# Attention over 32 memory slots and a bilinear FFN on one core: one written list orders every unit, column sums of exp(phi) on VectorE, all blocks in pairs of seven half products

## The chip, the core and the metric

The kernel runs on one core of a Trainium2 chip. A core has five engines with their own instruction streams, each in its own order: TensorE (PE in the profile, with its weight loads as PEld), VectorE (DVE), ScalarE (ACT), GpSimd (POOL) and SyncE (SP). They meet only at semaphores. Transfers between HBM and the on-chip memory (SBUF) run on 16 DMA engines that all queues share. Matrix products land in PSUM, eight banks in all. The metric is the device time in microseconds (us) of one execution; lower is better.

## What is computed

The reference, cut to what matters (8 batches, 8 heads, 576 tokens, head size 64, 32 memory slots, model width 512, inner width 1536):

```python
def _attn_ref(q, k, v, phi):
    a = phi - np.max(phi, axis=2, keepdims=True)
    a = np.exp(a)
    a = a / (np.sum(a, axis=2, keepdims=True) + 1e-09)
    k_m = np.einsum('bhsm,bhsd->bhmd', a, k)
    v_m = np.einsum('bhsm,bhsd->bhmd', a, v)
    scores = (1.0 / np.sqrt(q.shape[-1])) * np.matmul(q, k_m.transpose(0, 1, 3, 2))
    scores = scores - np.max(scores, axis=-1, keepdims=True)
    attn = np.exp(scores)
    attn = attn / (np.sum(attn, axis=-1, keepdims=True) + 1e-09)
    return np.matmul(attn, v_m)

def _moe_ref(x, w_a, w_b, w_out):        # x: the attention's output, 4608 tokens x 512
    return (x @ w_a) * (x @ w_b) @ w_out
```

The sum over tokens of exp(phi), one number for each memory slot, is the divisor of the first softmax. This text calls it the column sum.

## The kernel before

**Chain of a batch.** `exp_phi` (ScalarE) takes exp of phi. TensorE then sums k and v over tokens with these weights (`sums` for batches 0 and 1, line 270; `kv_sums` for batches 2 to 7, line 213). The column sums come out of the same products: `kv_sb` holds three planes, k, v and a third that is filled once with 1/16 (lines 155 and 168), so a product over plane 3 gives the column sum. `take_kv` or `sums` divides, the result is transposed, `scores` multiplies with q, `exp_scores`, `denominators` and `normalise` (later batches: `e_turn`, `token_sums`, `token_normalise`, `a_turn`) make the attention A. `fold` multiplies the v sums into both up weights, so that the FFN's up projections need only A: its PSUM results `pva` are cast into `vab` by `take_fold`.

**Up.** `up_half(b, i, hf, x)` makes one 128 x 288 tile of x @ w_a (x=0, PSUM `pa`, cast by ScalarE into `a_sb`) or of x @ w_b (x=1, PSUM `pb`, multiplied by VectorE with `a_sb` into `ht`). There are 8 x 12 x 2 such pairs. In batch 0 the casts lie in 20 slots of the `w_sums` buffer, which is not yet needed; later in a pool of 4.

**Down.** 36 blocks of 128 tokens are multiplied by `w_out`. The first four (`early_downs`, line 474) are done as they are: 12 products of 512 columns for each block. The other 32 go in 16 pairs (`two_downs`, line 518): a pair is a 2 x 2 block product made from seven half-size products instead of eight, each of 6 matmuls of 256 columns. It takes sums of weights (`sum_weights`, eight GpSimd operations, once) and four sums of tokens for each pair (`sum_tokens`; GpSimd, and VectorE for the last two pairs).

**Order.** The program is scheduled by hand: each engine runs its instructions in the order in which Python emits them. `chain` emits batches 0 and 1 from two strings, `period` attaches the chain units of batch b+1 to the up steps of batch b, and the class `Work` spreads the down matmuls over the up steps at an even rate. `settle` empties a started half product before units that take four banks. `fill` emits dummy products that keep TensorE busy while it has nothing to do: 98 of 128 columns and 10 of 512, all before 19 us. PSUM banks are given out in rotation, oldest first.

**Loads.** All of them but k of batch 0 are issued from GpSimd's queue, in order: phi, q, v of batch 0; the up weights in column ranges 0:256, 256:512, 512:1024, 1024:1536 (`load_wab`, lines 158 to 169); then `o0 p o1 k q0 q1 o2 o3 v0 v1 o4 o5`, that is the down weights in six parts between the loads of batch 1 (line 175). At most eight loads are in flight: an issue waits until the load eight places earlier has landed.

Of the kernel before, what the change touches and what calls it, by code (L numbers as in the profile page):

```python
# [14 lines left out]
CS = 16.0  # L15


@with_exitstack
def kernel(
# [54 lines left out]
    kv_sbs = [consts.tile([P, 3, NHP, NI * D], F16, name=f"kv_sb{t}") for t in range(2)]  # L74
# [80 lines left out]
    nc.vector.memset(kv_sbs[0][:, 2], 1.0 / CS)  # L155
    for x in halves:
        nc.vector.tensor_copy(out=kvs[0][:, 0, x], in_=k_f32[:, x])
    load_wab(0, 256)
    load_wab(256, 512)

    ones = consts.tile([P, 4, 32], F16, name="ones")
    nc.vector.memset(ones, 1.0)
    nc.gpsimd.affine_select(out=ones, in_=ones, compare_op=ALU.is_ge, fill=0.0, base=0,
                            pattern=[[-32, 4], [0, 32]], channel_multiplier=1)
    nc.gpsimd.affine_select(out=ones, in_=ones, compare_op=ALU.is_ge, fill=0.0, base=31,
                            pattern=[[32, 4], [0, 32]], channel_multiplier=-1)
    load_wab(512, 1024)
    nc.gpsimd.memset(kv_sbs[1][:, 2], 1.0 / CS)  # L168
    load_wab(1024, 1536)
    loads = {f"o{n}": lambda n=n: load_wo(n) for n in range(NFF // 2)}  # L170
    loads |= {"p": lambda: load_phi(1), "k": lambda: load_k(1)}
    for n, x in enumerate(halves):
        loads[f"q{n}"] = lambda x=x: load_q(1, x)
        loads[f"v{n}"] = lambda x=x: load_v(1, x)
    for x in "o0 p o1 k q0 q1 o2 o3 v0 v1 o4 o5".split():
        loads[x]()
# [11 lines left out]
    def units(b):  # L188
# [18 lines left out]
        def slot_sums(z):  # L207
            if z == 0:
                t["es"] = kvs[b][:, 2, 0, 0:2 * NHP * M].bitcast(F32).rearrange("p (c m) -> p c m", m=M)
            nc.vector.tensor_reduce(out=t["es"][:, 2 * z:2 * z + 2], in_=t["exp"][:, 2 * z:2 * z + 2].rearrange("p c i m -> p c m i"),  # L210
                                    axis=mybir.AxisListType.X, op=ALU.add)

        def kv_sums():

            given = "es" in t
            n = (3 - given) * D
            t["pkv"] = [banks.take([P, 2 * D + (1 if given else D)], F32, "pkv", hold=True) for _ in range(2)]
            for i in range(NI):
                for g in range(2):
                    for j in range(4):  # L220
                        r, hp = head(g, j)
                        nc.tensor.matmul(  # L222
                            t["pkv"][g][0][32 * j:32 * j + 32, 0:n],
                            t["exp"][64 * r:64 * r + 64, hp, i, :],
                            kvs[b][64 * r:64 * r + 64, 0:3 - given, hp, D * i:D * (i + 1)],
                            start=(i == 0),
                            stop=(i == NI - 1),
                            tile_position=(64 * r, 32 * j),
                        )
            for g in range(2 * given):  # L230
                for j in range(4):
                    r, hp = head(g, j)
                    nc.tensor.matmul(
                        t["pkv"][g][0][32 * j:32 * j + 32, 2 * D:2 * D + 1],
                        t["es"][64 * r:64 * r + 64, hp],
                        one_cs[64 * r:64 * r + 64],
                        start=True,
                        stop=True,
                        tile_position=(64 * r, 32 * j),
                    )  # L240
# [29 lines left out]
        def sums(g, x):  # L270
# [5 lines left out]
            part = (slice(0, 3, 2), slice(1, 2))[x]  # L276
            pk = banks.tile([P, 2 - x, D], F32, name="pk")
            for i in range(NI):
                for j in range(4):
                    r, hp = head(g, j)  # L280
                    nc.tensor.matmul(
                        pk[32 * j:32 * j + 32],
                        t["exp"][64 * r:64 * r + 64, hp, i, :],
                        kvs[b][64 * r:64 * r + 64, part, hp, D * i:D * (i + 1)],
# [4 lines left out]
            if x == 0:  # L289
                nc.vector.reciprocal(out=t["rphi"][:, g:g + 1], in_=pk[:, 1, 0:1])  # L290
            nc.vector.tensor_scalar(out=t["kvm"][:, g, x], in0=pk[:, 0], scalar1=t["rphi"][:, g:g + 1], scalar2=None,
# [12 lines left out]
        def scores(gs):  # L304
            if 0 in gs:
                t["E"] = mid.tile([P, 2, S], F16, name="E")
            if len(gs) > 1 and b > 2:
                work.settle()
# [70 lines left out]
        def fold(lo, hi, zs):  # L379
            if b not in vabs:  # L380
                vabs[b] = [mid.tile([P, 2, d_ff], F16, name=f"vab{x}") for x in range(2)]
            if len(zs) > 1 and b > 2:
                work.settle()
# [64 lines left out]
    def down_part(po, bank, cidx, lo, hi):  # L448
        pair, c = divmod(cidx, NI)
        for i in range(lo, hi):  # L450
            nc.tensor.matmul(po, ht[:, i, P * c:P * (c + 1)], wo_sb[:, i, :],  # L451
                             start=(i == 0), stop=(i == NFF - 1))
            if i == NFF - 1:
                banks.free(bank)
                o_sb = opool.tile([P, d_model], F32, name="o_sb")
                nc.scalar.mul(out=o_sb, in_=po, mul=1.0 / (CS * CS))
                for z in range(2):
                    slot = 2 * c + z
                    nc.sync.dma_start(out=out_rows[2 * pair + slot // NI, slot % NI],
                                      in_=o_sb[64 * z:64 * z + 64, :])  # L460
            yield

    def down(cidx):

        po, bank = banks.take([P, d_model], F32, "po", hold=True)
        yield from down_part(po, bank, cidx, 0, NFF)

    EARLY = 4

    def early_downs():  # L470

        pos = [banks.take([P, d_model], F32, "po", hold=True) for c in range(EARLY)]
        for n in range(NFF // 2):
            for c in range(EARLY):
                yield from down_part(*pos[c], c, 2 * n, 2 * (n + 1))

# [7 lines left out]
    def sum_weights():  # L487
        nc.gpsimd.tensor_copy(out=w_sums[:, 0, 0, 0:1], in_=attn[1][:, 1, S - 1:S])
        t = [w_sums[:, x] for x in range(4)]
        for out, in0, in1 in ((t[0], quarter(0, 1), quarter(0, 0)), (t[1], quarter(1, 1), t[0]),  # L490
                              (t[2], quarter(1, 1), quarter(0, 1)), (t[3], quarter(1, 0), t[1])):
            for x in range(2):
                sl = slice(KH // 2 * x, KH // 2 * (x + 1))
                nc.gpsimd.tensor_tensor(out=out[:, sl], in0=in0[:, sl], in1=in1[:, sl], op=ALU.subtract)
# [7 lines left out]
    def sum_tokens(cidx, engine):  # L502

        h_sums[cidx] = spool.tile([P, 4, KH, P], F16, name="h_sums")
        t = [h_sums[cidx][:, x] for x in range(4)]
        (a11, a12), (a21, a22) = ([tokens_of(cidx + y, x) for x in range(2)] for y in range(2))
        for out, in0, in1, op in ((t[0], a21, a22, ALU.add), (t[1], t[0], a11, ALU.subtract),
                                  (t[2], a12, t[1], ALU.subtract), (t[3], a11, a21, ALU.subtract)):
            engine.tensor_tensor(out=out, in0=in0, in1=in1, op=op)  # L509
            yield  # L510
# [7 lines left out]
    def two_downs(self, cidx):  # L518
        S1, S2, S4, S3 = (h_sums[cidx][:, x] for x in range(4))
# [3 lines left out]
        ends = cidx == PAIRED[-1]  # L523
# [22 lines left out]
        self.brim = True  # L546
# [11 lines left out]
        self.brim = False  # L558
# [7 lines left out]
        self.brim = True  # L566
# [7 lines left out]
        self.brim = False  # L574
# [14 lines left out]
    LEAD = 24  # L589
    PAIRED = range(EARLY, BLOCKS, 2)  # L590

    class Work:


        def __init__(self):
            self.todo = self.products()
            self.ready = self.done = self.summed = 0
            self.owed = self.rate = 0.0
            self.brim = False
            self.sums = self.add_up()  # L600
            self.next_sum = next(self.sums)

        def products(self):
            for cidx in PAIRED:
                yield from two_downs(self, cidx)

        def add_up(self):
            for n, cidx in enumerate(PAIRED):
                for x in range(4):
                    yield n, 7 * KH * n + KH * (x + 1)  # L610
                    if x == 0:
                        sums = sum_tokens(cidx, nc.gpsimd if n < len(PAIRED) - 2 else nc.vector)
                    next(sums)
            while True:
                yield len(PAIRED), 0

        def sum_ahead(self):
            while self.next_sum[0] < self.summed and self.next_sum[1] <= self.done + LEAD:
                self.next_sum = next(self.sums)

        def pull(self, n):
            for _ in range(min(n, self.ready - self.done)):
                self.owed -= 1.0
                self.sum_ahead()
                self.done += 1
                next(self.todo)

        def settle(self):

            while self.brim and self.done < self.ready:  # L630
                self.pull(1)

        def advance(self):
# [162 lines left out]
```

The softmax here doesn't subtract the row's maximum and nothing guards it: scores larger than these inputs give would overflow.

## Time and profile before

| | |
|---|---|
| time, median of 3 runs | 239.33 us (239.0 to 240.5) |
| span of the profiled execution | 237.2 us |
| TensorE busy | 227.1 us, 96% of the span |
| VectorE busy | 169.5 us, 71% |
| ScalarE busy | 153.7 us, 65% |
| GpSimd busy | 155.6 us, 66% |
| DMA | 37.27 MB, mean 157 GB/s |
| TensorE clock granted | 0.998 |

The span runs from the first to the last instruction; the measured time lies 2.1 us above it. TensorE's matmuls are pipelined, so busy time overstates what it does: the distance from one start to the next is the real price of one. Between 60 and 220 us the busy share is 99 to 100%. In that stretch VectorE is busy 13.2 to 16.6 us of each 20 us, ScalarE 12.1 to 16.6.

Durations that matter below, mean of one: `ht` multiply on VectorE 448 ns, `a_sb` cast on ScalarE 410 ns, `h_sums` on GpSimd 1640 to 1670 ns and on VectorE 550 ns, `w_sums` on GpSimd 1633 ns, `vab` casts 606 ns (ScalarE) and 683 ns (VectorE).

### The profile page before, as it was taken

The page shows a single profiled execution, that of the slowest core. Times are in us where ns is not written, and L with a number is a line of the kernel's source. Part 1 is how long each engine was busy: PE and PEld are TensorE (multiplying, and loading weights), DVE is VectorE, ACT ScalarE, POOL GpSimd, SP SyncE. Part 2 cuts the span into 40 slices and gives each one's busy share as a digit, 9 for nine tenths or more (in the row PEclk, how much of TensorE's full clock was granted, in tenths as well). Part 3 has the DMA queues.
Part 4 walks back from the last instruction along what each step waited for, and adds up shares of the span by engine and source line. Part 5 has one row for each costly group of instructions (what it writes and reads, how often), then busy time and mean ns, then how long its engine had stood idle before and what let it go on. Part 6 is the DMA issues. An engine that isn't in the chain of part 4 may idle for free.

```text
span 237.2 us, 7718 instructions
## 1 busy us (share of the span) xinstructions
PE 227.1 (96%) x3064; PEld 167.5 (71%) x3064; DVE 169.5 (71%) x415; ACT 153.7 (65%) x394; POOL 155.6 (66%) x132
## 2 busy tenths in 40 slices
PE   7888998999999999999999999999999999999993
PEld 7545563455756877868777877877878687888882
DVE  4646874368949958969776995779786877766642
ACT  2276761559699589786778458776776777555330
POOL 7954244589979969392799699692939265956001
PEclk9999999999999999999999999999999999999999
DMA  6999999999982999944499857997063342212146
GB/s 231 236 198 206 211 252 207 243 220 275 229 182 50 219 262 252 220 100 92 80 248 238 153 123 171 211 203 99 6 137 59 82 104 37 56 34 67 38 101 155
DMA packets 38436, 37.27 MB, mean 157 GB/s; under 512 B 14688, under 2 KB 32480, under 8 KB 38400
## 3 DMA queue, kind: packets, MB, share of 16 engines
q0 software_dynamic: 19264, 23.14, 52.5%
q1 hardware_dynamic: 18624, 12.85, 24.3%
q10 hardware_dynamic: 512, 0.79, 1.0%
q8 instruction: 24, 0.39, 0.7%
q14 instruction: 12, 0.10, 0.1%
HBM read 42.47 MB, written 9.44 MB: 219 GB/s over the span
## 4 chain that ended last, share of the span: by engine, by line
PE 76%; DMA 14%; POOL 5%; ACT 2%; issue 1%; DVE 1%; DVEq 0%; POOLq 0%
PE py L527 17%; PE pa L655 17%; PE pb L655 17%; PE pv L527 8%; DMA wa_sb<-in_moe_w_a_dram 6%; DMA wo_sb<-in_moe_w_out_dram 6%; PE pva L389 5%; PE px L527 4%; PE po L451 3%; PE pkv L222 2%; DMA kvT<-rep 2%; PE pscore L318 1%; POOL wb_sb L100 1%; POOL wa_sb L99 1%; POOL kv_sb L168 1%
## 5 line engine op out<-in xcount | busy, mean ns | idle before, releaser
L666 DVE TENSOR_TENSOR ht<-a_sb,pb 128x288 f16<-128x288 f16 x168 | 72.3, 448 | 33.5 <-ACT a_sb L663 23.7
L655 PEld LDWEIGHTS <-vab 128*128 128x128 f16 x768 | 73.1, 98 | 22.1 <-issue 5.3
L663 ACT CAST a_sb<-pa 128x288 f16<-128x288 f32 x168 | 65.9, 410 | 30.8 <-PE pa L655 26.4
L655 PE MATMUL pa<-A,vab 128*128 128x288 f16 x384 | 75.8, 286 | 0.0
L655 PE MATMUL pb<-A,vab 128*128 128x288 f16 x384 | 75.3, 286 | 0.1
L509 POOL TENSOR_TENSOR h_sums<-ht 128x768 f16<-128x768 f16 x28 | 46.7, 1670 | 23.1 <-DVE ht L666 23.1
L527 PEld LDWEIGHTS <-h_sums 128*128 128x128 f16 x384 | 36.7, 98 | 9.2 <-issue 3.0
L402 ACT CAST vab<-pva 128x512 f16<-128x512 f32 (+1 forms) x60 | 31.9, 575 | 7.5 <-PE pva L389 7.1
L527 PEld LDWEIGHTS <-ht 128*128 128x128 f16 x288 | 27.9, 98 | 6.1 <-issue 1.3
L527 PE MATMUL py<-w_sums,h_sums 128*128 128x256 f16 x192 | 30.2, 273 | 0.0
L402 DVE CAST vab<-pva 128x512 f16<-128x512 f32 (+1 forms) x44 | 26.7, 635 | 3.7 <-PE pva L389 3.6
L509 POOL TENSOR_TENSOR h_sums<-h_sums,ht 128x768 f16<-128x768 f16 x14 | 23.4, 1668 | 0.9
L509 POOL TENSOR_TENSOR h_sums<-ht,h_sums 128x768 f16<-128x768 f16 x14 | 23.0, 1640 | 0.9
L331 ACT ACTIVATE E<-pscore 128x288 f16<-128x288 f32 x32 | 10.7, 416 | 10.6 <-PE pscore L318 10.5
L527 PE MATMUL pv<-w_sums,h_sums 128*128 128x256 f16 x96 | 16.2, 273 | 0.0
L527 PE MATMUL py<-wo_sb,ht 128*128 128x256 f16 x96 | 16.2, 273 | 0.0
L534 ACT ACTIVATE u<-py 128x256 f32<-128x256 f32 x32 | 12.5, 391 | 5.7 <-PE py L527 5.2
L527 PE MATMUL px<-wo_sb,ht 128*128 128x256 f16 x96 | 15.9, 273 | 0.0
L527 PE MATMUL py<-w_sums,ht 128*128 128x256 f16 x96 | 15.2, 273 | 0.1
L527 PE MATMUL pv<-wo_sb,h_sums 128*128 128x256 f16 x96 | 14.4, 273 | 0.0
L196 ACT ACTIVATE exp_sb<-phi_sb 128x576 f16<-128x576 f32 x16 | 10.9, 699 | 5.2 <-DMA phi_sb<-in_phi_dram 5.2
L205 DVE STREAM_TRANSPOSE qT<-q_sb 128x288 f32<-128x288 f32 x32 | 14.1, 460 | 0.2 <-DMA q_sb<-in_q_dram 0.2
(71 smaller groups left out, 264.7 us busy)
## 6 DMA issues: line engine op xcount, KB each, us to landing
out_dram<-o_sb SPq DMA_DIRECT2D x68, 128.0 KB, 3.0
phi_sb<-in_phi_dram POOLq DMA_DIRECT2D x8, 576.0 KB, 7.9
kv_sb<-in_v_dram POOLq DMA_DIRECT2D x7, 576.0 KB, 11.2
kv_sb<-in_k_dram POOLq DMA_DIRECT2D x7, 576.0 KB, 11.8
q_sb<-in_q_dram POOLq DMA_DIRECT2D x6, 576.0 KB, 14.2
wo_sb<-in_moe_w_out_dram POOLq DMA_DIRECT2D x6, 256.0 KB, 12.7
q_sb<-in_q_dram POOLq DMA_DIRECT2D x4, 288.0 KB, 11.0
wa_sb<-in_moe_w_a_dram POOLq DMA_DIRECT2D x2, 512.0 KB, 13.9
```

The source lines that it names most:

```text
L196: nc.scalar.activation(out=t["exp"][:, 2 * z:2 * z + 2, :, :], in_=phis[b][:, 2 * z:2 * z + 2, :].rearrange("p c (i m) -> p c i m", m=M), ...
L205: nc.vector.transpose(out=t["qT"][:, hp, :].bitcast(F32), in_=qs[b][:, hp, :].bitcast(F32))
L331: nc.scalar.activation(out=Ev[:, g, :, z, :], in_=pss, func=AF.Exp, scale=1.0 / (8.0 * CS))
L389: nc.tensor.matmul(t["pva", lo, z][g][0][32 * j:32 * j + 32, 0:hi - lo], t["kvT"][64 * r:64 * r + 64, 4 + g, M * j:M * j + M], w_sbs[z][64 ...
L402: engine_copy(out=vabs[b][z][:, g, lo:hi], in_=pva[:, 0:hi - lo])
L451: nc.tensor.matmul(po, ht[:, i, P * c:P * (c + 1)], wo_sb[:, i, :], start=(i == 0), stop=(i == NFF - 1))
L509: engine.tensor_tensor(out=out, in0=in0, in1=in1, op=op)
L527: nc.tensor.matmul(po, lhs[:, i], rhs[:, i], start=first and i == 0, stop=i == KH - 1, skip_group_check=not first)
L534: nc.scalar.mul(out=x, in_=po, mul=scale)
L655: nc.tensor.matmul(ps, vabs[b][x][:, g, P * i:P * (i + 1)], attn[b][:, g, HALF * hf:HALF * (hf + 1)], start=(g == 0), stop=(g == 1))
L663: nc.scalar.copy(out=a_sbs[b, i, hf], in_=ps)
L666: nc.vector.tensor_tensor(out=ht[:, i, t0:t0 + HALF], in0=a_sbs.pop((b, i, hf)), in1=ps, op=ALU.mult)
```

## The change

- The third plane of `kv_sb` and its two fills are gone. `slot_sums` on VectorE (two reductions for each batch) makes the partial column sums `es` in float32, and `counts`, new, has TensorE add them up: eight matmuls of one column for each batch, float32 by float32. `kv_sums` streams 128 columns instead of 192, `sums` 64 instead of 128 in its first half.
- `early_downs` is gone: all 36 blocks go in 18 pairs.
- `chain`, `period`, `Work` and `settle` are gone. `PLAN` lists every unit: `f`/`F` dummy products of 128/512 columns, `w`, `o`, `p`, `k`, `v`, `q` loads, `a`/`b` up tiles, `T`/`V` sums of weights on GpSimd/VectorE, `h`/`g` sums of tokens on GpSimd/VectorE, `d` down matmuls, and units of the chains such as `0ks0`.
- Loads: up weights in the order 0:256, 512:1024, 256:512, 1024:1536, with half of batch 1's q ahead of the last; then batch 1; then the down weights as o2 o0 o1 o3 o5 o4.
- The casts of batch 0 use the pool of 4.

```diff
+PLAN = """
+f1 F1 f2 f1 f2 f3 f2 f3 F1 O f3 f1 f1 0exp0 f2 f1 w0:256 f3 f3 f1 F1 0ps0 f4 0qt0 f78 f1 f2 f1 f2 0exp1 f2 0ps1
+0ks0 f3 f2 0qt1 0ks1 0kt0 f2 w512:1024 w256:512 F3 0s0 F2 f2 f1 0e0 0kt1 F3 0qt2 0qt3 F3 0vs1 0den00 f1 f1 f3
+0den01 f4 F1 0nr00 0vs0 0s1 f3 0nr01 0vt1 f2 0vt0 0e1 0den10 q1.0 f3 f4 0hv0a 0hv0b 0hx0b 0v1a 0nr10 0hx0a f2 f2
+0den11 F2 F2 f3 0x1a f1 f5 0nr11 a0.0.0 a0.1.0 w1024:1536 b0.0.0 a0.6.1 0v1b b0.1.0 a0.0.1 0hv1a 0x1b f4 b0.0.1
...
+g16.2 d1 g16.3 g17.0 d4 g17.1 d51 h17.2 d7 h17.3 d19
+"""
...
-    kv_sbs = [consts.tile([P, 3, NHP, NI * D], F16, name=f"kv_sb{t}") for t in range(2)]
+    kv_sbs = [consts.tile([P, 2, NHP, NI * D], F16, name=f"kv_sb{t}") for t in range(2)]
...
-                t["es"] = kvs[b][:, 2, 0, 0:2 * NHP * M].bitcast(F32).rearrange("p (c m) -> p c m", m=M)
+                t["es"] = small.tile([P, NHP, M], F32, name="es")
             nc.vector.tensor_reduce(out=t["es"][:, 2 * z:2 * z + 2], in_=t["exp"][:, 2 * z:2 * z + 2].rearrange("p c i m -> p c m i"),
                                     axis=mybir.AxisListType.X, op=ALU.add)
...
+        def counts(pk, g, col):
+            for j in range(4):
+                r, hp = head(g, j)
+                nc.tensor.matmul(
+                    pk[32 * j:32 * j + 32, col:col + 1],
+                    t["es"][64 * r:64 * r + 64, hp],
+                    one_cs[64 * r:64 * r + 64],
+                    start=True,
+                    stop=True,
+                    tile_position=(64 * r, 32 * j),
+                )
...
-            if len(gs) > 1 and b > 2:
-                work.settle()
...
         if x == 0:
-            if b == 0:
-                n = (2 * i + hf) % 20
-                a_sbs[b, i, hf] = spare[:, HALF * n:HALF * (n + 1)]
-            else:
-                a_sbs[b, i, hf] = apool.tile([P, HALF], F16, name="a_sb")
+            a_sbs[b, i, hf] = apool.tile([P, HALF], F16, name="a_sb")
...
+    for x in PLAN.split():
+        arg = x[1:]
+        if x[0] in "fF":
+            fill(int(arg), P if x[0] == "f" else 512)
+        elif x == "O":
+            fill_ones()
+        elif x[0] in "wopkvq":
+            issue(x)
...
+        elif x[0] in "TV":
+            sum_weights(int(x[1]), int(x[2]), nc.gpsimd if x[0] == "T" else nc.vector)
+        elif x[0] in "hg":
+            n, y = arg.split(".")
+            sum_tokens(int(n), int(y), nc.gpsimd if x[0] == "h" else nc.vector)
+        elif x[0] == "d":
+            for _ in range(int(arg)):
+                next(down)
+        else:
+            us[int(x[0])][arg]()
```

What each engine is given, before and after: TensorE 48 products of 512 columns and 672 of 256 become none and 756; dummy products 98 (128 columns) and 10 (512) become 199 and 22; 64 float32 matmuls of one column are new. VectorE gets 16 reductions `es`, 21 sums of tokens instead of 8, four of the eight sums of weights, and six more `o_sb` additions; it loses one fill of a plane. GpSimd keeps 51 of 56 sums of tokens and four sums of weights, and loses one fill of a plane.

## The prediction

> **What bounds the kernel now.** I read the shares by slice first, then the waits of TensorE, then TensorE's and GpSimd's timelines up to 62 us, then busy time by stretch.
>
> ```profile
> PE   7888998999999999999999999999999999999993
> DMA  6999999999982999944499857997063342212146
> ...
> PE pva L389 <- DMA wa_sb<-in_moe_w_a_dram: 0.8, 2, 0.7
> PE pk L281 <- ACT exp_sb L196: 0.7, 1, 0.7
> PE po L451 <- DMA wo_sb<-in_moe_w_out_dram: 0.5, 1, 0.5
> ```
>
> A slice is 5.9 us. TensorE is at 9 in every slice but the last from the eighth (41.5 us) on. The transfers are full for the first eleven slices (to 65 us). TensorE's named waits are sub-microsecond, so there are two stages: a start that the loads pace, and a long stretch in which TensorE's own work is the time. For that stretch I need the price of a matmul, the distance between starts in the timeline:
>
> ```profile
> 220.87 0.82 PE L527 MATMUL pv<-wo_sb,h_sums 128*128 128x256 f16 x6
> 221.52 0.82 PE L527 MATMUL py<-w_sums,h_sums 128*128 128x256 f16 x6
> ...
> 22.61 0.67 PE L655 MATMUL pa<-A,vab 128*128 128x288 f16 x4
> 23.11 0.65 PE L655 MATMUL pb<-A,vab 128*128 128x288 f16 x4
> ```
>
> Six of 256 columns take 0.65 us (0.109 each); four of 288 take 0.49 (0.1225 each). In the same way one of 512 columns takes 0.215, a dummy of 128 about 0.054, a packed `pkv` of 192 columns 0.0107, `pk` of 64 columns 0.0097, `pva` of 512 columns 0.035, `pscore` 0.0128.
>
> In the start, GpSimd waits at each load until the load eight places earlier has landed, so its waits are a clock of landings:
>
> ```profile
> 22.51 0.70 POOL L90 DMA_DIRECT2D q_sb<-in_q_dram  x1 [1.83 <-DMA wa_sb<-in_moe_w_a_dram]
> 25.05 0.71 POOL L90 DMA_DIRECT2D q_sb<-in_q_dram  x1 [1.85 <-DMA wb_sb<-in_moe_w_b_dram]
> 27.57 0.70 POOL L104 DMA_DIRECT2D wo_sb<-in_moe_w_out_dram  x1 [1.81 <-DMA wa_sb<-in_moe_w_a_dram]
> 30.10 0.71 POOL L104 DMA_DIRECT2D wo_sb<-in_moe_w_out_dram  x1 [1.83 <-DMA wb_sb<-in_moe_w_b_dram]
> ```
>
> The two 512-column pieces of the up weights land at 22.5 and 25.1, the last range at 27.6 and 30.1: 2.5 us for 512 KB, in the order of issue. The other waits give v of batch 0 at 14.6, the first range at 15.9 and 17.3, 1.3 us for 256 KB, 1.5 for a phi and 2.8 for a k or v. Nothing in the change shortens these bytes.
>
> **What the Trainium skill says.** "TensorE: Matmul & The Clock Gate", section "Back-to-back issue gap", gives N/2.4 + 2.5 ns; for 288 columns 122.5 ns, which the trace agrees with. "FP8 and Floating Point Precision", section "TensorE Precision Notes", says true FP32 takes 4 passes through the array; "TensorEngine Tiling (Array Packing)", section "Instruction Overhead", says about 60 cycles for any small matmul. No row of this profile shows a float32 matmul, so these two price `counts` below. "VectorE: DVE Perf Modes", "The perf-mode tier table", holds `tensor_reduce` to its slowest mode; the trace agrees: 812 ns for 640 elements of 16 bits.
>
> **The change part by part.** I anchor on TensorE's first up tile of batch 1: both versions have then done all of batch 0's ups and batch 1's chain. Before, it starts at 48.25 us (timeline), with 37 of the 48 early down products already done.
>
> *Start.* Loads in the new order, by the clock above: first range 15.9 and 17.3, then 512:1024 at 19.8 and 22.3, 256:512 at 23.6 and 24.9, half of q1 26.3, last range 28.8 and 31.3, phi 32.8, k1 35.6, rest of q1 37.2, v1 40.0, down weights by six steps of 1.3 until 47.8. GpSimd's dropped fill (2.0 us) brings issues forward, not landings. Now TensorE's new order, at the prices above, with the dummies cold at 107 ns up to about 4 us: its first product over 512:1024 comes up at about 17.4, and waits for its 19.8. Behind it stand 17 dummies of 128 and 4 of 512 columns (1.8 us with one `pD`) before the first up tile, at about 21.8; before it was 17.81. What the dummies were to fill is by then over, so they are paid in full. The later folds wait only a few tenths. `pk` of batch 1 comes up at 34.9 and waits for k1 at 35.6. From there to the first up tile the chain takes 9.3 us at best (batch 0 before: 8.54 to 17.81): 44.9. So the anchor comes 48.25 - 44.9 = **3.35 us earlier**, but without down products.
>
> *Remaining work at the anchor.* Before: 672 up products (82.3), 672 half-size products (73.2), 11 early ones (2.4), six `pkv` groups (432 x 0.0107 = 4.6), folds and the rest 15.3: 177.9 us. After: ups the same, 756 half-size (82.4), `pkv` of 128 columns at about 0.0085 (3.7), 48 `counts`, folds and rest 14.9: 183.3 plus `counts`. All pairs cost 84 x 0.109 = 9.2 us where 48 x 0.215 = 10.3 stood, so 1.1 is saved over the run; but 7.9 of the old 10.3 lay in the start, in time that TensorE could not use otherwise. That is the core of my forecast. **+5.4 us**, without `counts`.
>
> *Counts.* Lower end 0.03 us each (four passes packed as `pkv` is), upper 0.21 (my estimate from the two pages: four passes of 25 ns, each with its own 27 ns load of 32 columns, none overlapped). I take 0.08: 48 x 0.08 = **+3.8**; ends +1.4 and +10.1. The 16 of batches 0 and 1 lie in the start.
>
> *Waits inside the long stretch.* Before, from the anchor to the last matmul's end (233.4) are 185.2 us, with 177.9 of work: 7.3 lost, by the timeline 1.6 of it up to 60.6, some 2.5 up to 80, 1.5 after 220, the rest in crumbs. The list weaves the downs between ups with care and may save half of the first two; but VectorE gets 12 reductions at 0.74 (812 x 576/640), 13 sums of tokens and four of weights at 0.55, six additions at 0.42: 20.8 us. It was busy 16.6 of 20 us between 80 and 120, and each `pb` bank waits for it. I take 5.0 lost: **-2.3**; ends 2 and 9 lost. Dropping `settle` leaves four-bank units beside a started half product; that belongs to the same bound. ScalarE changes by under 1 us (four casts of 0.59 go, eight of 0.39 come). GpSimd loses 17 us, which frees nothing TensorE waits for, though its load issues now stand behind sums: k, v of batch 2 land by about 59.5 and are wanted at 62. Later loads hide under TensorE: between 100 and 220 us the DMA engines are busy 0.59 of the time. The outputs are the same 9.4 MB; SyncE's queue issues as many stores.
>
> *Nothing:* the slots for batch 0's casts (at most four are open in the list, as the pool has) and the removed plane (its fill on VectorE ends before k arrives at 5.8).
>
> *Sum.* -3.35 + 5.4 + 3.8 - 2.3 = **+3.6 us**. The profiled execution has 237.2 span and the median lies 2.1 above: 239.33 + 3.6, about **243 us**. That case's own range is 239 to 247.
>
> **Rivals.**
> - *The list fits and the dummies stand only where TensorE would wait.* Then no wait is added: list of work and dummies from 1.26 on, 223.4 us, plus 2 lost, plus the 3.8 us of tail and 2.1 outside: 232.6. For it: the tails of both orders are alike and the work is 1 us less. Against: the product over 512:1024 at 17.4 against its landing at 19.8. Partly true, it gives 233 to 237, faster. It decides if the start ends by about 40 us with the dummies all hidden.
> - *`counts` run one after another* at 0.21: 243 + 6.3 = 249. For it: their weight load belongs to the matmul. Against: neighbours lie in different parts of the array, and `pkv` overlaps there some eightfold.
> - *VectorE becomes the bound* from 60 to 220 us: at 16.6 + about 2.2 of each 20 us it is over 90% and waits no longer hide; 4 to 8 us more lost, 247 to 251.
> - *The start's debt is won back*: `counts` at 0.03 and 3 us lost give 239 - about no change.
>
> **How the numbers follow.** My case 0.40, fits 0.20, counts 0.13, VectorE 0.12, won back 0.15. The range must reach into the fast case and to the slow ones: 236 to 250. A run of this kernel tells about 1% from no change (236.9 to 241.7). Faster 0.21; same 0.21 (won back, and the low edge of mine); slower 0.58.
>
> **What would show it.** In the profile after: the first up tile of batch 0 near 21.8 us and of batch 1 near 45; a named wait of `pva` for `wa_sb` of over 1 us; the distance of the `counts` matmuls; TensorE at 9 in all slices from the ninth on; the last matmul near 237. I am wrong if batch 1's ups start by 42, if `counts` cost nothing and the stretch after the anchor has under 3 us of waits, or if VectorE's queue opens gaps in it.

## The result, and the profile after

| | before | after |
|---|---|---|
| time, median | 239.17 us (238.97 to 240.5, 4 runs) | 250.94 us (250.73 to 251.35, 4 runs) |
| ratio | | 1.049 (1.046 to 1.052) |
| span of the profiled execution | 237.2 us | 249.6 us |
| TensorE's first up tile of batch 0 | 17.81 us | 24.10 us |
| TensorE's first up tile of batch 1 (the anchor) | 48.25 us | 48.38 us |
| TensorE's last matmul ends near | 233.4 us | 245.7 us |

The changed kernel is 11.8 us slower. The direction was forecast, the size was not: 243 was said, and the end of the range was 250.

The page of the kernel after, shares by slice (a slice is now 6.2 us), with VectorE's row:

```profile
PE   7989998794899999999999999999999999999993
DVE  1725799889999999998989799999876889777452
...
DMA  6999999999970999994699669432702532020354
```

TensorE is at 4 in the tenth slice (56.2 to 62.4 us) and at 8 in the one behind it. VectorE is at 9 or 8 in every slice but one from the sixth to the twenty-ninth; its busy time went from 169.5 to 202.4 us. The waits of TensorE, largest first (total us, times, longest):

```profile
PE pb L627 <- DVE ht L634: 3.8, 2, 3.2
PE py L556 <- DVE o_sb L567: 1.5, 1, 1.5
PE pT L366 <- issue: 1.4, 1, 1.4
```

Before, the waits shown were of 0.8 us at most, and most of them for transfers. Now the first two are for VectorE, and one of 3.2 us stands out. No wait of `pva` for `wa_sb` is among them. TensorE's timeline around the wait of 3.2 us (start, us, then the group; in brackets the idle time ahead of it and what ended it):

```profile
55.99 0.41 PE L627 MATMUL pa<-A,vab 128*128 128x288 f16 x2
59.55 0.41 PE L627 MATMUL pb<-A,vab 128*128 128x288 f16 x2 [3.15 <-DVE ht L634]
...
62.27 0.68 PE L627 MATMUL pb<-A,vab 128*128 128x288 f16 x2
62.75 0.68 PE L627 MATMUL pa<-A,vab 128*128 128x288 f16 x2
```

After the hole two products of 288 columns take 0.48 us from one start to the next, twice the 0.245 that they take elsewhere: the hole is followed by a stretch at half clock, and the clock granted is 0.50 from 60.26 to 63.67. What VectorE did meanwhile, in its own timeline:

```profile
54.77 4.36 DVE L523 TENSOR_TENSOR w_sums<-wo_sb 128x768 f16<-128x768 f16 x1
59.05 1.17 DVE L634 TENSOR_TENSOR ht<-a_sb,pb 128x288 f16<-128x288 f16 x3
60.15 2.12 DVE L523 TENSOR_TENSOR w_sums<-wo_sb,w_sums 128x768 f16<-128x768 f16 x1
```

One sum of weights takes 4.36 us, another 2.12. I had priced one at 0.55. Behind the first stand the `ht` multiplies that free TensorE's `pb` banks. GpSimd in the same microseconds:

```profile
53.11 1.64 POOL L523 TENSOR_TENSOR w_sums<-wo_sb,w_sums 128x768 f16<-128x768 f16 x1
54.69 0.77 POOL L148 DMA_DIRECT2D kv_sb<-in_v_dram  x1
55.47 1.65 POOL L523 TENSOR_TENSOR w_sums<-wo_sb 128x768 f16<-128x768 f16 x1
57.07 1.64 POOL L540 TENSOR_TENSOR h_sums<-ht 128x768 f16<-128x768 f16 x1
58.65 0.77 POOL L153 DMA_DIRECT2D q_sb<-in_q_dram  x1
```

GpSimd's own sums keep their 1.64 us. VectorE's ends at 59.13, 0.4 us after GpSimd's last sum has ended (58.71): as it seems, it did nothing until then. VectorE's sums over the whole run, grouped by shape (count, total us, mean ns):

```profile
L523 DVE TENSOR_TENSOR w_sums<-wo_sb 128x768 f16<-128x768 f16 x1 | 4.4, 4361 | 0.0
L523 DVE TENSOR_TENSOR w_sums<-wo_sb,w_sums 128x768 f16<-128x768 f16 x3 | 5.2, 1725 | 0.0
L540 DVE TENSOR_TENSOR h_sums<-ht,h_sums 128x768 f16<-128x768 f16 x7 | 6.3, 896 | 0.0
L540 DVE TENSOR_TENSOR h_sums<-ht 128x768 f16<-128x768 f16 x11 | 6.8, 626 | 0.0
```

And the page's group of the new reductions:

```profile
L276 DVE TENSOR_REDUCE es<-exp_sb 128x64 f32<-128x576 f16 x16 | 18.0, 1134 | 1.2 <-ACT exp_sb L262 1.2
```

1134 ns each, where I took 740: 18.0 us in all. Busy time by stretch, from 60 to 80 us and from 140 to 160 us after the change (stretch and its length; then TensorE's matmuls, its weight loads, VectorE, ScalarE and GpSimd with their counts; granted clock; DMA share; GB/s):

```profile
60.00:80.00 20.00, 18.09 (x260) 13.05 (x258) 19.93 (x40) 11.00 (x30) 9.66 (x8) 0.91 0.74 147
140.00:160.00 20.00, 19.97 (x286) 15.65 (x284) 19.43 (x48) 12.54 (x34) 10.99 (x9) 1.00 0.80 154
```

From 60 to 80 us VectorE is busy 19.93 of 20 us, and TensorE's clock is down to 0.91. From 140 to 160 it is busy 19.43 us, and TensorE has no gap. If the matmuls that the trace has in each stretch are priced as in the prediction (`counts` at what they took, small folds and transposes roughly) and taken from its length, TensorE loses 8.8 us between the anchor and 80 us (before: 3.9), and 3.5 us from 80 us to its last matmul (before: 3.5). Of the 8.8, some 1.7 is the half clock. So a full VectorE cost time only up to 80 us, where single operations of it also stretched over several microseconds; the hundred microseconds from 80 on, with 16.9 to 19.4 busy of each 20, cost nothing that shows.

### The profile page after: what moved, and what is told of

It is laid out like the page before. It is cut to its first block, busy times and chain, and to the rows that moved or that the text cites. A ratio compares the mean times of both kernels' runs of the same rounds, so it can differ in the third digit from the quotient of the medians.

```text
span 249.6 us, 8282 instructions
## 1 busy us (share of the span) xinstructions
PE 234.8 (94%) x3341; PEld 180.6 (72%) x3341; DVE 202.4 (81%) x453; ACT 153.2 (61%) x398; POOL 138.0 (55%) x120
## 4 chain that ended last, share of the span: by engine, by line
PE 86%; DVE 8%; issue 4%; ACT 0%; DVEq 0%
PE py L556 18%; PE pb L627 18%; PE pa L627 17%; PE pv L556 9%; PE pw L214 8%; PE pva L452 5%; PE px L556 4%; DVE ht L634 3%; DVE es L276 2%; PE pscore L383 2%; PE pD L406 1%; PE pkv L298 1%; PE pk L347 1%; DVE vab L465 1%; PE pT L366 1%
## 5 line engine op out<-in xcount | busy, mean ns | idle before, releaser
L631 ACT CAST a_sb<-pa 128x288 f16<-128x288 f32 x192 | 72.7, 406 | 42.5 <-PE pa L627 30.2
L634 DVE TENSOR_TENSOR ht<-a_sb,pb 128x288 f16<-128x288 f16 x192 | 80.3, 445 | 18.6 <-PE pb L627 13.4
L540 POOL TENSOR_TENSOR h_sums<-ht 128x768 f16<-128x768 f16 x25 | 41.2, 1655 | 37.5 <-DVE ht L634 35.4
L556 PEld LDWEIGHTS <-h_sums 128*128 128x128 f16 x432 | 42.1, 98 | 10.1 <-issue 2.2
L556 PE MATMUL py<-w_sums,h_sums 128*128 128x256 f16 x216 | 38.0, 275 | 0.0
L214 PE MATMUL pw<-warm 128*128 128x128 f16 (+1 forms) x221 | 22.8, 251 | 1.9 <-DVE warm L183 1.3
L540 POOL TENSOR_TENSOR h_sums<-ht,h_sums 128x768 f16<-128x768 f16 x11 | 18.3, 1664 | 8.5 <-DVE h_sums L540 8.2
L214 PEld LDWEIGHTS <-warm 128*128 128x128 f16 x221 | 15.8, 105 | 8.4 <-issue 4.8
L276 DVE TENSOR_REDUCE es<-exp_sb 128x64 f32<-128x576 f16 x16 | 18.0, 1134 | 1.2 <-ACT exp_sb L262 1.2
L556 PE MATMUL pv<-wo_sb,h_sums 128*128 128x256 f16 x108 | 19.0, 273 | 0.0
## 6 DMA issues: line engine op xcount, KB each, us to landing
wa_sb<-in_moe_w_a_dram POOLq DMA_DIRECT2D x2, 512.0 KB, 12.1
```

The costliest lines, as they stand in the source:

```text
L214: nc.tensor.matmul(pw[:, :cols], warm[:, :P], warm[:, :cols], start=True, stop=True)
L556: nc.tensor.matmul(po, lhs[:, i], rhs[:, i], start=first and i == 0, stop=i == KH - 1, skip_group_check=not first)
L631: nc.scalar.copy(out=a_sbs[b, i, hf], in_=ps)
L634: nc.vector.tensor_tensor(out=ht[:, i, t0:t0 + HALF], in0=a_sbs.pop((b, i, hf)), in1=ps, op=ALU.mult)
```

## The experiments

My theory on seeing this: *VectorE's and GpSimd's operations keep each other out when both read two operands from SBUF, so sums moved to VectorE beside GpSimd's cost far more than 0.55 us; the long reductions do the rest.* Rivals: the late work alone (no early blocks, 5.4 us) with a start that came no earlier; the dummies; VectorE's load as such, whatever is on it. Each kernel below was timed against the kernel before on the same chip (239.0 to 239.1 us there).

**1. All sums up to 68 us on VectorE** (`a_allv`). In the list of the changed kernel, the four sums of weights on GpSimd and its five sums of tokens up to there go to VectorE, so GpSimd runs none beside them, but for the last sum of weights:

```diff
-h0.3 ... h0.1 ... T01 ... T00 ... h0.2 ... T10 ... T20 h1.0 ... h1.1
+g0.3 ... g0.1 ... V01 ... V00 ... g0.2 ... V10 ... V20 g1.0 ... g1.1
```

> The kernel after, but the four sums of weights and all sums of tokens that GpSimd has up to the last sum of weights (about 68 us) go to VectorE, so VectorE gets nine more operations there and GpSimd none. If the two engines exclude each other while both read SBUF (collision theory), the sums on VectorE fall from 1.3 to 4.4 us to 0.55 each, the 3.2 us wait of pb for ht goes, and the time falls by 3 to 6 us, to 245 to 248. If VectorE simply has too much to do (load theory), nine more operations of 0.55 make it 3 to 5 us slower, 254 to 256.

Measured: 249.98 us (248.48 to 250.29), ratio 1.0435 (1.0399 to 1.0472). VectorE's sums of weights, by shape:

```profile
L520 DVE TENSOR_TENSOR w_sums<-wo_sb,w_sums 128x768 f16<-128x768 f16 x4 | 3.5, 884 | 0.0
L520 DVE TENSOR_TENSOR w_sums<-wo_sb 128x768 f16<-128x768 f16 x4 | 2.2, 551 | 0.0
```

Four of them now take 551 ns where one took 4361. In the other group three take 0.55 us; the fourth took 1.88, from 64.61 us on, beside GpSimd's first sum (64.44 to 66.07). That is what exclusion predicts. But the time fell by only 1 us, less than I had expected: nine more operations on VectorE keep it at 19.02 of 20 us from 60 to 80, and TensorE waits 2.2 us for `o_sb` and 2.1 for `ht`. Priced as above, TensorE still loses 7.9 us between the anchor and 80 us. The stretched sums are not the whole cause: VectorE has no room for its own share either, which run 4 tests.

**2. All sums of weights on GpSimd** (`a_vt`). The opposite edit:

```diff
-V21 ... V11 ... V31 ... V30
+T21 ... T11 ... T31 ... T30
```

> The kernel after with the four sums of weights of VectorE moved to GpSimd. Collision and load theory both expect the 3.2 us wait of pb for ht to go. Collision theory: VectorE gets back 9.6 us, not the 2.2 that four operations of 0.55 cost, and the time falls by 2 to 5 us; GpSimd's own 1.64 each put later sums of tokens back by up to 6.5 us, which can take part of it. Load theory: VectorE gets back 2.2 us and the time falls by at most 1.

Measured: 252.91 us (252.12 to 253.54), ratio 1.0575 (1.0548 to 1.0603). Both views missed it. TensorE's waits:

```profile
PE py L553 <- POOL w_sums L520: 6.1, 1, 6.1
```

At 1.64 us each, GpSimd finishes the eight sums so late that a half product waits 6.1 us for them. The split between the two engines had a reason: neither engine alone is in time.

**3. The changed kernel without `es`** (`a_noes`). The column sums come from a third plane of 1/16 again, as before; `slot_sums` and `counts` are gone. The list is otherwise the same.

```diff
-    kv_sbs = [consts.tile([P, 2, NHP, NI * D], F16, name=f"kv_sb{t}") for t in range(2)]
+    kv_sbs = [consts.tile([P, 3, NHP, NI * D], F16, name=f"kv_sb{t}") for t in range(2)]
-... 0ps0 ... 0ps1 ... 7ps0 ... 7ps1 ...
```

> The kernel after with the column sums from the plane of ones again (no reductions on VectorE, no float32 products, the two fills of planes back). VectorE gets back 16 x 1.13 = 18 us, 4.5 of them before the first up tile of batch 1. If VectorE's queue is what holds TensorE there and between 48 and 80 us (theory), the first up tile of batch 1 comes 1 to 3 us earlier and the time falls by 4 to 7 us. If the reductions are hidden (rival), TensorE only pays its wider products and the time is within 1 us.

Measured: 253.18 us (252.06 to 254.66), ratio 1.0571 (1.0545 to 1.0598): slower than with them. TensorE waited 10.1 us at one place, for fold casts that stood in VectorE's queue behind this operation:

```profile
46.73 10.53 DVE L426 TENSOR_TENSOR A<-E,R 128x576 f16<-128x576 f16 x1
```

An operation of the same kind takes 0.46 us in the kernel before. GpSimd at that time:

```profile
46.58 3.24 POOL L532 TENSOR_TENSOR w_sums<-wo_sb 128x768 f16<-128x768 f16 x2
49.77 1.63 POOL L549 TENSOR_TENSOR h_sums<-ht,h_sums 128x768 f16<-128x768 f16 x1
51.36 1.62 POOL L532 TENSOR_TENSOR w_sums<-wo_sb,w_sums 128x768 f16<-128x768 f16 x1
52.93 0.76 POOL L144 DMA_DIRECT2D kv_sb<-in_v_dram  x1
53.71 1.65 POOL L532 TENSOR_TENSOR w_sums<-wo_sb 128x768 f16<-128x768 f16 x1
55.31 1.63 POOL L549 TENSOR_TENSOR h_sums<-ht 128x768 f16<-128x768 f16 x1
```

Six sums run nearly back to back, and VectorE's product of two SBUF tiles ends (57.26) when they have. The product comes up when it did in the changed kernel (46.73 us for 46.77), where it took 1.11; but GpSimd's sums of weights begin at 46.58 instead of 48.30 us, because the sum of tokens on VectorE that GpSimd waits for starts at 43.57 instead of 44.95. So less work on VectorE brought GpSimd's sums over that product. The run says nothing of the cost of `es`; it shows how dear the exclusion can be.

**4. Without `es`, and with the sums of 1** (`a_noes_allv`): edits 1 and 3 together.

> The kernel after with both edits: column sums from the plane of ones, and all sums of weights and tokens up to about 68 us on VectorE, so that GpSimd can't hold VectorE up there. In the run with the plane of ones alone one multiply of A took 10.5 us beside GpSimd's sums. Collision theory: that hole goes, and what the reductions cost in the list shows at last: 243 to 246, 4 to 6 us under the run with the sums on VectorE alone (249.98). Rival (the reductions are hidden, the hole was theirs by another way): 249 or more.

Measured: 245.38 us (245.37 to 245.85), ratio 1.0269 (1.0251 to 1.0288), as expected. The hole is gone. Against run 1, `es` and `counts` cost 4.6 us in this list; the anchor comes 0.9 us earlier (47.35 for 48.22), the rest is won after it. Priced as above, TensorE loses 4.2 us between the anchor and 80 us, about the 3.9 of the kernel before. So the two together, sums beside GpSimd's and the reductions, made the new losses of that stretch; taken away in this order, the reductions with `counts` were the larger part.

**5. Also without the dummies after batch 0's first divisors** (`a_combo`): every `f` and `F` behind `0den11` leaves the list.

```diff
-0den11 F2 F2 f3 0x1a f1 f5 0nr11 a0.0.0 a0.1.0 ...
+0den11 0x1a 0nr11 a0.0.0 a0.1.0 ...
```

> The same without the dummies that follow the unit 0den11 (the ones that stand behind the wait for the columns 512:1024; those before, which warm the clock, stay). If they are paid in full, another 1 to 2.5 us go: 241 to 245. If they fill waits, no change within 0.7 us. Under 239.1 it would beat the kernel before; the late work of 5.4 us says that it does not.

Measured: 242.31 us (241.31 to 242.69), ratio 1.0128 (1.0102 to 1.0154): those dummies, 45 of 128 and 7 of 512 columns, last 3.9 us by the prediction's prices, and 3.1 of that was paid. TensorE reaches batch 1 much earlier now:

```profile
44.11 0.30 PE L636 MATMUL pa<-A,vab 128*128 128x288 f16 x1
```

44.11 us, where the prediction had 44.9 for the changed kernel. What is left above the kernel before, 3.2 us, is the late work (6.4 here, since the wide `pkv` is back and `counts` are gone) less this start (4.1) with some 0.9 of waits; that split is by sum, not by a run.

**6. The changed kernel without dummies behind `0ks0`** (`a_nofill`): 80 of 128 and 19 of 512 columns, 8.4 us, all else as it was.

> The kernel after without the 80 dummies of 128 and 19 of 512 columns that follow the first ks unit (8.4 us of TensorE at full clock). If they are paid in full (the step of the prediction), the first up tile of batch 1 comes 2 to 4 us earlier and the time falls by as much. If they stand where TensorE would wait anyway (rival), waits take their place, the time is within 1 us, or up to 3 us longer if the granted clock drops.

Measured: 249.04 us (247.37 to 250.79), ratio 1.0415 (1.036 to 1.047). Removing 8.4 us of dummies gained 1.9: the wait of `pb` for `ht` is still there with 3.4 us, and TensorE's mean clock fell from 0.990 to 0.972: its first up tiles of batch 0 ran at half clock (0.50 from 15.61 to 25.85 us). The dummies were paid in part; they also kept the clock up.

**7. The kernel before with all blocks in pairs** (`b_allpairs`), and **8. the same with a dummy of 512 columns in place of each early product** (`b_dummies`), to see what the early blocks were worth:

```diff
-    EARLY = 4
+    EARLY = 0
...
-    work.plan(S + HALF, 10)
+    work.plan(S + HALF, 8)
     ups(half_steps(1, 1, 4), slots(2, ...))
+    work.pull(2 * 7 * KH - work.done)
```

The change from 10 to 8 and the last line bring the pairs' products forward and finish two pairs by the end of batch 1.

> The kernel before, but with no early down blocks: all 36 blocks go in 18 pairs, with its own even spreading; nothing else is changed. TensorE gets 84 x 0.109 = 9.2 us of late work in place of 10.3 us of which 7.9 lay in the start. If the start is paced by loads and chain (my theory), the start shortens by at most 3.5 us and the time rises by 4 to 8 us. If the early blocks held up the start by their whole 8 us (rival), the time is the same or 1 us lower.

> The kernel before with all 36 blocks in pairs, and in the place of each early down product a dummy of the same 512 columns, so that TensorE's clock and its start are as before. Against the run without dummies (257.7) it tells how much of the 18.6 us was the clock. Theory: 9.2 us of half-size products come on top of an unchanged start, 247 to 251. Rival, that the even spreading or the later sums of weights make the loss: 253 or more.

Measured: 257.67 us (257.25 to 258.87), ratio 1.0784 (1.0756 to 1.0812), and 257.65 us (256.85 to 258.32), ratio 1.0773 (1.0742 to 1.0803). Both far above what I expected. In 7 the clock was at 0.65 from 40 to 60 us, and I suspected that; 8 keeps it at 1.00 there and takes as long, so the clock there is not the cause. TensorE's waits in 8:

```profile
PE pscore L318 <- DMA kvT<-rep: 3.8, 1, 3.8
PE py L527 <- POOL h_sums L509: 1.9, 3, 0.8
PE pv L527 <- POOL h_sums L509: 1.4, 2, 0.9
```

GpSimd is busy 18 of 20 us from 60 to 100 and its sums of tokens come late for the two pairs more; a unit of the next chain finds no work to hide its transfer. So dropping the early blocks in the old, hand-spread order, with these edits, costs more than its 9.2 us of products (84 of 256 columns). The two runs don't isolate the late work of the changed kernel, whose list is spread otherwise.

**9. The kernel before with `es`** (`b_es`), reductions right ahead of the products, and **10. placed where `exp_sb` is ready** (`b_es2`, batches 2 to 7):

```diff
-        u["kv"] = one(kv_sums)
+        u["kv"] = lambda: (slot_sums(0), slot_sums(1), kv_sums())
```

> The kernel before with the column sums of batches 2 to 7 by VectorE and 48 float32 products of one column (batches 0 and 1 and the plane of ones stay). VectorE pays 12 x 1.13 = 13.6 us, TensorE saves some 6 x 0.2 us of pkv and pays 6 x 0.3 for the counts. If VectorE's added work comes through to TensorE (theory), the time rises by 1.5 to 5 us; if it stays hidden (rival), it is within 0.7 us of before.

> The kernel before with the column sums of batches 2 to 7 on VectorE as in the run at 261.2, but each reduction placed behind the exp that it needs, two slots ahead of the sums over k and v, not right in front of them. If the 22 us came from the place (TensorE waiting for two reductions in each batch), the time falls to 241 to 246. If the reductions themselves are the cost, it stays over 252.

Measured: 260.99 us (259.43 to 261.37; a fourth run, not counted, took 264.0), ratio 1.0898 (1.0858 to 1.0938), and 248.01 us (246.36 to 248.24), ratio 1.0356 (1.0322 to 1.039). The first only shows a bad place: TensorE waited 13.8 us, twelve times, for reductions that had just been issued. The second still waits:

```profile
PE pkv L233 <- DVE kv_sb L210: 4.0, 4, 1.5
```

12 reductions, put as well as I could into the old order, cost 8.9 us. Under the changed list they cost less (run 4).

**11. Two sums of weights on VectorE in the kernel before** (`b_vsum`):

```diff
-                nc.gpsimd.tensor_tensor(out=out[:, sl], in0=in0[:, sl], in1=in1[:, sl], op=ALU.subtract)
+                engine = nc.vector if out is t[2] else nc.gpsimd
+                engine.tensor_tensor(out=out[:, sl], in0=in0[:, sl], in1=in1[:, sl], op=ALU.subtract)
```

> The kernel before with two of its eight sums of weights on VectorE, put at the same place, while GpSimd runs the other six. They need nothing but the down weights. Collision theory: the two take 2 to 10 us of VectorE in place of 1.1, and the time rises by 1 to 6 us. Rival (no exclusion): 0.55 us each, no change within 0.7 us.

Measured: 239.09 us (238.89 to 239.4), ratio 1.000 (0.9991 to 1.0009). VectorE's timeline tells why it decides nothing:

```profile
48.43 1.01 DVE L495 TENSOR_TENSOR w_sums<-wo_sb 128x768 f16<-128x768 f16 x2
```

Both had ended at 49.44, before GpSimd began its own sums (49.57). So the same two operations were emitted two and four half steps later, in the middle of GpSimd's six (**12**, `b_vsum2`):

```diff
-    ... "d3+y1+hv1a+hx1a hv1b+y3+hx1b - - - y3+v1+x1a+x1b - -"
+    ... "d3+y1+hv1a+hx1a hv1b+y3+hx1b z0 - z1 y3+v1+x1a+x1b - -"
```

Here `z0` and `z1` are the two halves of the third sum on VectorE.

> The kernel before, with two of its eight sums of weights on VectorE, placed so that they come up about 51 to 54 us, inside the stretch in which GpSimd works through its six other sums back to back (49.1 to 58.8 us). Theory (a VectorE operation with two 16-bit operands in SBUF and a GpSimd operation keep each other out): at least one of the two takes 1.6 to 5 us instead of 0.55, and the ht multiplies behind it come late, with a wait of pb for ht of 1 to 4 us; time 240 to 243. Rival (the long sums of the changed kernel have another cause, such as the transfers that run then): 0.55 us each, no change, 239.

Measured: 240.25 us (240.05 to 240.46), ratio 1.0053 (1.004 to 1.0067). VectorE:

```profile
50.76 1.82 DVE L500 TENSOR_TENSOR w_sums<-wo_sb 128x768 f16<-128x768 f16 x1
52.50 0.81 DVE L672 TENSOR_TENSOR ht<-a_sb,pb 128x288 f16<-128x288 f16 x2
53.23 1.26 DVE L500 TENSOR_TENSOR w_sums<-wo_sb 128x768 f16<-128x768 f16 x1
```

and GpSimd:

```profile
48.93 3.23 POOL L496 TENSOR_TENSOR w_sums<-wo_sb 128x768 f16<-128x768 f16 x2
52.12 7.05 POOL L496 TENSOR_TENSOR w_sums<-wo_sb,w_sums 128x768 f16<-128x768 f16 x4
```

The same operation takes 0.5 us while GpSimd has no sum at work (run 11) and 1.82 and 1.26 while it has; the first ends at 52.58, 0.4 us after GpSimd's second sum. GpSimd pays as well: four of its sums take 7.05 us where four took 6.43 in run 11. The two `ht` multiplies between, with one operand in PSUM, keep their 0.4 us. Nothing but the place differs between 11 and 12, and the transfers, the rival, are alike: 219 GB/s from 48 to 50 us in run 11, 209 and 206 from 50 to 54 in run 12. So the exclusion is shown. TensorE's wait of `pb` for `ht` is 0.7 us, less than I expected. The new place and the exclusion together cost 1.2 us for two operations; the run doesn't part them.

No version found is faster than the kernel before. What was not tried: the early blocks put back into the list.

## Why the prediction was wrong

The sum was -3.35 (start) + 5.4 (late work) + 3.8 (`counts`) - 2.3 (waits) = +3.6. Measured on the profiled executions, span against span: +12.4. The 17 dummies of 128 columns that I counted ahead of the first up tile are 17 in all, four of them of 512; the 1.8 us given for them are about right.

- **What bounds it: right.** From about 80 us on, TensorE's own work is the time in both kernels, and the losses are alike (3.5 us in both).
- **Start: wrong, -3.35 became +0.1.** The first up tile of batch 0 came at 24.10, not 21.8, and the anchor at 48.38, not 44.9. Of the 3.5 us between the two anchors, 2.3 lie ahead of the first tile. Transfers are not what held it. The first half of columns 512:1024 landed when I had said, and the product over it came up two microseconds later, so no wait for `wa_sb` shows and that sign was missed too:

```profile
19.84 0.74 POOL L145 DMA_DIRECT2D kv_sb<-in_k_dram  x1 [1.84 <-DMA wa_sb<-in_moe_w_a_dram]
21.90 0.40 PE L452 MATMUL pva<-wa_sb,kvT 64*32 64x512 f16 x8
```

What lies ahead of it are two stalls named "issue" (1.4 us at 13.71, 0.3 at 19.84) and a chain that was slower than its prices. The products of k for batch 1 come up at 38.15 instead of 34.9, and from there the chain takes 10.2 us, with another stall of 0.8, instead of 9.3. The three stalls are 2.5 us, for which the prediction had no term. Runs 4 and 5 bring the anchor to 47.35 and 44.11: the term's size could be had, and `es` and the dummies behind the first divisors stood in its way.
- **Late work: +5.4, unrefuted.** The products in the trace behind the anchor are as computed, and the best list (run 5) stays 3.2 us above the kernel before although its anchor comes 4.1 us earlier. No run isolates the term: 7 and 8 changed the waits along with it.
- **`counts`: too dear, +3.8 was about +2.0.** From 73.01 us on, batch 2's eight matmuls stand in the timeline as 16 rows:

```profile
73.01 0.33 PE L282 MATMUL pkv<-one_cs,es 64*32 64x1 f32 x16
73.28 0.28 PE L556 MATMUL pv<-w_sums,h_sums 128*128 128x256 f16 x1
```

The next matmul starts 0.27 us later: 0.034 each, close to my lower end. The six batches take 0.26 to 0.50, 1.97 in all. The Trainium skill's page "FP8 and Floating Point Precision", section "TensorE Precision Notes", gave four passes; the trace shows two rows for each matmul. The load of 27 ns in my upper end stands on neither of the two pages that I named for it. The rival "`counts` run one after another" is out.

- **Waits: this is the step that failed.** I took 5.0 us lost after the anchor, with the two ends 2 and 9; after the anchor 197.4 us passed for 185.3 of work (183.3 and 2.0 of `counts`), so 12.1 were lost: the term is +4.8 against before's 7.3, not -2.3. It is what remains, so with it the sum must come near the 12.4 measured: 0.1 + 5.4 + 2.0 + 4.8 = 12.3. The count of matmuls in the trace gives nearly the same (8.8 + 3.5 lost), and what is new lies between the anchor and 80 us; run 4 takes it away. I had let VectorE's added 20.8 us hide under TensorE and even took waits off. Two prices under that step were wrong. A sum on VectorE stood at 0.55, from a row of the tail of the kernel before, where GpSimd is idle. The Trainium skill's page "SBUF — State Buffer", section "Who interferes with whom", says that a VectorE instruction with two SBUF inputs contends with a GpSimd instruction that reads SBUF, and that the port pair they share is an exclusive lock; I didn't use it, and the trace agrees (4.36 for 0.55 us). And `es` stood at 0.74, scaled by elements from another reduction; it takes 1.134.
- **Rivals.** "VectorE becomes the bound", 247 to 251, named the right engine and the right size, and I gave it 0.12. Its place was wrong: it spoke of all of 60 to 220 us, and VectorE was over 90% busy in much of it without cost; what cost time was 54 to 80 us. Why a VectorE at 19.02 of 20 us costs much there (run 1) and one at 19.4 nothing later stays open. The sign "TensorE at 9 from the ninth slice on" fails there, in the tenth and the eleventh, and nowhere later before the last. "The list fits" and "the debt is won back" are out.
- **Range.** It ended at 250, the time is 250.94. My own case with 9 us lost ends at 247; nothing in it let the start fail at the same time.

By edits the 11.8 us came back as 1.0 (sums up to 68 us on one engine), 4.6 (`es` and `counts`), 3.1 (late dummies) and 3.2 that remain. The order of these edits matters: with `es` and `counts` taken away first, the kernel was 2.2 us slower than with them (run 3).

## What to carry to other kernels

Price an operation by a row that was taken beside the same neighbours: 0.55 us from a tail with an idle neighbour was 1.3 to 4.4 us beside a busy one, and what is dear is the queue behind it. Before work is moved to an engine that is off the path, look at what that engine releases and how long its longest single operation can get; the busy share alone doesn't tell, as 19.4 of 20 us without a cost and 19.0 (run 1) and 19.9 with one show. An edit that removes load can bring a blocking neighbour's work forward onto an operation, so one removal is no measure of what it removed.

## What the runs showed of the hardware

- VectorE and GpSimd meet not only at semaphores: their operations on SBUF kept each other out (run 12). A VectorE operation that is kept out by GpSimd can wait for several of its operations in a row: through six sums and a DMA issue of 0.76 us between them (10.53 us, run 3), though in run 12 it came in between two sums. What decides this is open.
- A hole of 3.15 us in TensorE's work was followed by 3.41 us at half clock (0.48 us for 0.245), which began 0.7 us after the work had resumed. The Trainium skill's page "TensorE: Matmul & The Clock Gate", section "What's actually happening", has the clock drop after at least one idle window of about 3.4 us; here less was enough. In run 5 the clock was at half for the same 3.4 us from 44.91 on, and no hole in the 5 us ahead was longer than 0.9 us. How much work in a window keeps the clock up is not shown.
- TensorE's "issue" stalls in the start, for which the trace names no semaphore:

```profile
13.71 0.22 PE L366 MATMUL pT<-ident,kvm 128*32 128x128 f16 x1 [1.36 <-issue]
44.28 0.72 PE L347 MATMUL pk<-kv_sb,exp_sb 64*32 64x64 f16 x66 [0.80 <-issue]
```

Counted over matmuls and weight loads, about 445, 701 and 1467 of them lie ahead of the stalls here, and in run 5 about 699 and 1466: distances near multiples of 256. The page of the kernel after lists a queue of kind "instruction" that moved 0.43 MB in 26 packets, 16,384 bytes each. All 19 such stalls over 0.25 us, in the seven runs that have any, end 1.2 to 1.5 us after one of these packets has landed (here at 12.30, 18.37 and 42.77 us). The kernel before has no such stall: it comes to its matmul behind 445 others at 14.33 us, and the packet had landed at 11.16. So TensorE seems to wait for its own instructions there, while the DMA engines are full; no run changed only that.
